# Attention and a state-space convolution in one planned kernel: planner slack, the last chunk in halves, and more filler matmuls

## The chip, the cores and the metric

The kernel runs on one core of a Trainium2 chip. The metric is device time in microseconds. The core has five engines with an instruction queue each: TensorE (PE, with its weight loads shown as PEld), VectorE (DVE), ScalarE (ACT), GpSimd (POOL) and SyncE (SP). They meet through semaphores. Here POOL and SP issue the DMAs.

## The reference

Two results are mixed by a gate for each of 2048 tokens: `g * a + (1 - g) * b`, where `g` is the sigmoid of `x · gate_w`. All inputs are bf16.

```python
# a: attention, 16 heads of 28, one shared key and value head, D = 448
q = (x @ wq).reshape(B, S, H, Dh).transpose(0, 2, 1, 3)
k = x @ wk
v = x @ wv
p = softmax(einsum("bhqd,bkd->bhqk", q, k) * Dh ** -0.5)
a = einsum("bhqk,bkd->bhqd", p, v).transpose(...).reshape(B, S, H * Dh) @ wo
# b: a long convolution of u = x with K, 448 channels, 256 complex states each
P = exp((dt * A)[:, :, None] * arange(L))
K = einsum("dn,dnl,dn->dl", Cc, P, dt * Bc).real
b = causal_convolution(u, K) + u * Dskip
```

Both parts are applied to the same `x`. The reference convolves through FFTs, the kernel multiplies Toeplitz matrices.

## The kernel before

**Attention.** There are 16 steps, called heads here: four blocks of 512 queries by four groups of four heads. A head has 64 score tiles (16 key blocks by 4 heads), each 128x512, so 1024 tiles in all. `qk` (L1110) makes three or two tiles at a time in PSUM, ScalarE takes their exponential into a ring `expT` (L1126), and `pv` (L1135) multiplies four tiles by the values; a column of ones gives the softmax denominators. ScalarE has this stream and little else.

**Normalisation.** When a head is complete, `norm` has VectorE copy the accumulator out of PSUM into `acc` (L1025, two buffers). Then POOL issues four DMAs that gather the denominators into `denT`, VectorE takes the reciprocal (L1030), POOL issues one DMA to a DRAM scratch `R_scratch` and four that broadcast it back into `rdenB`, and VectorE multiplies `acc` by it into `onT` (L1034). The last head goes through matmuls instead (L1042, L1053). `outp` and `tail` project `onT` and `fold` adds into the output `O` (L1016).

**Convolution.** The 448 channels are 14 chunks of 32, in blocks of 2, 4, 4 and 4 chunks. For a block, `masters` makes powers in float32 and stores bf16 copies in `mbf`. For a chunk, `tables` makes powers by doubling on VectorE, in five levels (L885 to L891: two products, a subtraction and an addition each), then a real factor `rho` (L898), their product (L902) and a negation (L907). `kgen` multiplies the tables on TensorE (L924) into 32 rows of K, VectorE adds the skip term and casts to `kstg` (L934, L937), and POOL issues nine DMAs into `KP_scratch`. `tload` then reads, from SP, one Toeplitz tile `T` for each four channels (1072 KB, a ring of five, called groups 0 to 111 in the text). `conv` runs for 16 channels at a time, so twice a chunk, over four groups: 128 matmuls (L970), a product with the gate into `cst` on VectorE (L979), a shift and transpose by matmuls (L990), and an addition into `O` (L998).

**What sets the order.** `Prog.schedule` plans all instructions ahead with its own estimate of each one's length, takes the one that can start soonest, and fixes one order for each engine. Engines then run in that order: an instruction that waits holds everything behind it on its engine. A score matmul has priority: other TensorE work is not planned into the last `MARGIN` ns before ScalarE needs new scores. `SLACK` moves the planned ready time of low priority work that depends on another engine, which changes its place in the order and adds no wait. Afterwards `fill` puts matmuls on zeros into TensorE's planned idle time wherever a moving window's score of planned activity is under `SCORE`.

Of the kernel before, what the change touches and what calls it, by code (L numbers as in the profile page):

```python
# [28 lines left out]
BW = 64 * BC  # L29
MC = 1280 + 5 * 64  # L30
NTR = 5
RING = 15
NON = 5
# [38 lines left out]
class Op:  # L72
    __slots__ = ("i", "eng", "fn", "ns", "lat", "deps", "pr", "lock", "unlock", "slot", "ndma",
                 "count", "vc", "end", "comm", "extra", "mode", "st")


class Prog:
# [5 lines left out]
    MARGIN = 120.0  # L83
# [11 lines left out]
    def op(self, eng, fn, ns, rd=(), wr=(), pr=0, lat=None, lock=None, unlock=None, comm=None, mode="f", st=None):  # L95
# [4 lines left out]
        o.mode = mode  # L100
# [43 lines left out]
    def schedule(self):  # L144
# [20 lines left out]
        while done < n:  # L165
# [68 lines left out]
            for j in succ[i]:  # L234
                need[j] -= 1
                x = ops[j]
                if x.eng == e and o.slot is None and e == "pe":
                    t = free[e]
                elif x.eng == e and o.slot is None:
                    t = free[e] + self.SAME[e]  # L240
                else:
                    t = end + self.SEM_NS
                    if x.pr >= (1.2 if x.eng == "pe" else 2):
                        t += self.SLACK.get(x.eng, 0.0)
# [104 lines left out]
def on(i):  # L349
    return i % NON  # L350


class Kernel:
# [3 lines left out]
    SCORE = 13.8  # L357
# [77 lines left out]
    def consts(self):  # L435
# [6 lines left out]
        dm(V(self.kstg, 0, 256), 0.0, 170, ["kst"])  # L442
# [33 lines left out]
    def loads(self):  # L476
# [41 lines left out]
        for k in range(2, 6):  # L518
# [7 lines left out]
               (448, 128), "pad", rd=["kst"], wr=["pad"], pr=3)  # L526
# [164 lines left out]
    def prep_params(self):  # L691
# [8 lines left out]
        tc = lambda j: spot[j][0].v(0, P, spot[j][1], [[D, 2], [32, NC], [1, 32]])  # L700
# [41 lines left out]
        ap9 = self.seed.v(0, P, 2 * W2, [[32, 2], [64, NC], [1, 32]])  # L742
        pg.op("act", lambda e: e.activation(ap9, tc(0), AF.Exp, scale=-2.0), 950, rd=[K(0)], wr=["sq"], pr=0.5)
        zc = lambda c: self.seed.v(0, P, c * W2, [[32, 2], [64, NC], [1, 32]])
        wc = lambda c: self.seedw.v(0, P, c * W2, [[32, 2], [64, NC], [1, 32]])
# [20 lines left out]
        for s in range(2):  # L766
            o = s * LO + 32 * EW
            for comp, val in ((0, 1.0), (1, 0.0)):
                pg.op("dve", lambda e, o=o, comp=comp, val=val: e.memset(self.tab.v(0, P, o + comp * BLK, [[1, 64]]), val), 70,
                      wr=[("lo", s, 0)] + (xd if s == 0 else ["sz0", "sz1", "sq", "sw0", "sw1"]), pr=3)  # L770
# [39 lines left out]
    def masters(self, b):  # L810
# [22 lines left out]
        for k in range(11):  # L833
# [12 lines left out]
            off = k * 256 if k < 5 else (k - 6) * 256 + 64  # L846
            dv(lambda e, k=k, off=off: e.tensor_copy(mbf.v(0, P, off, [[128, 2], [MC, nb], [1, 64]]), both(k, [[64, nb], [1, 64]])),
               2 * w, keys(k) + tp, [("mb", k)], 1.92)
        qq = self.sz.v(0, P, 2 * BW, [[1, w]])
        qd = self.sz.v(0, P, 2 * BW, [[64, nb], [1, 64]])  # L850
        for lv in range(5):
            if lv:
                dv(lambda e: e.tensor_tensor(qq, qq, qq, ALU.mult), w, ["sqq"], ["sqq"])
            dv(lambda e, lv=lv: e.tensor_copy(mbf.v(0, P, 1280 + 64 * lv, [[MC, nb], [1, 64]]), qd), w, ["sqq"] + tp, [("mq", lv)], 1.92)

    def tables(self, c):
# [4 lines left out]
        mo = ci * MC  # L861
        tab, mbf, tmp, rho = self.tab, self.mbf, self.tmp, self.rho
        pr = 50 + 2 * c

        def vo(fn, n, rd, wr, rate=1.92):
            pg.op("dve", fn, el(n, rate), rd=rd, wr=wr, pr=pr)
        mk = lambda lv: [("mb", lv), ("mb", lv + 6)]
        lk = lambda l: ("lo", s, l)
        vo(lambda e: e.tensor_copy(tab.v(0, P, lo + 31 * EW, [[BLK, 2], [1, 64]]), mbf.v(0, P, mo, [[128, 2], [1, 64]])),
           128, [("mb", 0), lk(0)], [lk(1)])  # L870
        vo(lambda e: e.tensor_copy(tab.v(0, P, lo + 31 * EW + 64, [[BLK, 2], [1, 64]]),
                                   self.sw.v(0, P, ci * 64, [[BW, 2], [1, 64]])),
           128, ["sbw", "sbw2", lk(0)], [lk(2)])
        done = [lk(1), lk(2)]
        for lv in range(5):
            w = 1 << lv
            m = mo + lv * 256
            n = w * EW
            so, do = lo + (32 - w) * EW, lo + (32 - 2 * w) * EW
            src = tab.v(0, P, so, [[BLK, 2], [EW, w], [1, EW]])  # L880
            dst = tab.v(0, P, do, [[BLK, 2], [EW, w], [1, EW]])
            mr = mbf.v(0, P, m, [[0, 2], [0, w], [1, EW]])
            mi = mbf.v(0, P, m + 128, [[0, 2], [0, w], [1, EW]])
            kr, ki = lk(3 + 2 * lv), lk(4 + 2 * lv)
            vo(lambda e, dst=dst, src=src, mr=mr: e.tensor_tensor(dst, src, mr, ALU.mult), 2 * n, done + mk(lv), [kr, ki])  # L885
            tb, to, tk = (tmp, 0, "tmp") if lv < 4 else (tab, FM, "Fm")
            vo(lambda e, src=src, mi=mi, w=w, tb=tb, to=to: e.tensor_tensor(  # L887
                tb.v(0, P, to, [[w * EW, 2], [EW, w], [1, EW]]), src, mi, ALU.mult), 2 * n, done + mk(lv), [tk])
            vo(lambda e, do=do, n=n, tb=tb, to=to: e.tensor_tensor(  # L889
                tab.v(0, P, do, [[1, n]]), tab.v(0, P, do, [[1, n]]), tb.v(0, P, to + n, [[1, n]]), ALU.subtract), n, [tk, kr], [kr])  # L890
            vo(lambda e, do=do, n=n, tb=tb, to=to: e.tensor_tensor(  # L891
                tab.v(0, P, do + BLK, [[1, n]]), tab.v(0, P, do + BLK, [[1, n]]), tb.v(0, P, to, [[1, n]]), ALU.add), n, [tk, ki], [ki])
            done = done + [kr, ki]
        vo(lambda e: e.tensor_copy(rho.v(0, P, 31 * 64, [[1, 64]]), mbf.v(0, P, mo + 1280, [[1, 64]])), 64,
           [("mq", 0)], ["tmp"])
        for lv in range(5):
            w = 1 << lv
            vo(lambda e, w=w, lv=lv: e.tensor_tensor(rho.v(0, P, (32 - 2 * w) * 64, [[64, w], [1, 64]]),  # L898
                                                     rho.v(0, P, (32 - w) * 64, [[64, w], [1, 64]]),
                                                     mbf.v(0, P, mo + 1280 + 64 * lv, [[0, w], [1, 64]]), ALU.mult), w * 64,  # L900
# [319 lines left out]
```

## Time and profile before

| what | us |
|---|---|
| median of 13 runs | 560.27 |
| lowest and highest | 550.6, 566.21 |
| the profiled execution, its own time | 556.17 |
| its span, first to last instruction | 554.4 |
| mean granted TensorE clock in it | 0.892 |

The profile is of one execution. Busy times of an engine are unions of its instructions' times; a group's mean is the length of one instruction; "idle before" is the engine's idle time just before such instructions, with what ended most of it. These groups matter:

```profile
L1126 ACT ACTIVATE expT<-psS 128x1536 bf16<-128x1536 f32 (+1 forms) x410 | 468.9, 1324 | 28.4 <-PE psS L1110 27.0
L1110 PE MATMUL psS<-qT,kT 29*128 29x512 bf16 x1024 | 176.8, 422 | 29.6 <-ACT expT L1126 25.1
L885 DVE TENSOR_TENSOR tab<-tab,mbf 128x256 bf16<-128x256 bf16 (+4 forms) x70 | 68.7, 981 | 1.0
L902 DVE TENSOR_TENSOR tab<-tab,tmp 128x4096 bf16<-128x4096 bf16 x14 | 32.0, 2288 | 0.3
```

Read the first line so: 410 exponentials kept ScalarE busy 468.9 us, the mean one took 1324 ns, and ScalarE was idle 28.4 us before them, 27.0 of that until scores from L1110 were ready. The DMA issues, with the median time from issue to landing:

```profile
T<-KP_scratch SPq DMA_DIRECT2D x112, 1072.0 KB, 9.5
rdenB<-R_scratch POOLq DMA_DIRECT2D x60, 64.0 KB, 5.6
KP_scratch<-kstg POOLq DMA_DIRECT2D x112, 16.0 KB, 3.6
```

### The profile page before, as it was taken

To read this page: it belongs to the slowest core of one execution; us is meant where nothing else is said; L and a number is where in the kernel's file an instruction comes from. 1 tells how busy PE (TensorE), PEld (TensorE's weight loads), DVE (VectorE), ACT (ScalarE), POOL (GpSimd) and SP (SyncE) were. 2 spreads that over 40 slices of the span, in tenths; PEclk is the share of its full clock that TensorE was granted. 3 is DMA by queue.
4 is the path that set the end of the run, shared out by engine and by line. 5 is a ranking of instruction groups with operands and counts; after the bars stand their busy time and mean duration, and the time that the engine had idled before them with its cause. 6 is when DMAs were issued, how large, how long until landed. Compare 5 with 4: busy or idle time off the path is not lost.

```text
span 554.4 us, 19990 instructions
## 1 busy us (share of the span) xinstructions
PE 484.1 (87%) x9080; PEld 259.4 (47%) x9080; DVE 460.9 (83%) x870; ACT 483.4 (87%) x427; POOL 139.9 (25%) x281
## 2 busy tenths in 40 slices
PE   6789979889797989989998989988998989899852
PEld 5545344446354544545354544444454534445541
DVE  7979799998989899999989898998999798911230
ACT  2899899999999989999998989999899989879700
POOL 2000111512214244024213144213313141415000
PEclk9975588799799999999787998899799999869985
DMA  8931100594767778998774878897793979877994
GB/s 237 271 115 48 31 21 4 155 402 146 281 253 270 314 287 290 350 379 312 281 301 138 354 278 316 266 411 310 241 422 80 371 261 352 309 273 246 343 424 160
DMA packets 37628, 142.81 MB, mean 258 GB/s; under 512 B 9888, under 2 KB 20680, under 8 KB 23208
## 3 DMA queue, kind: packets, MB, share of 16 engines
q1 hardware_dynamic: 27656, 135.29, 65.0%
q0 software_dynamic: 8352, 6.09, 4.6%
q8 instruction: 71, 1.16, 0.8%
q10 hardware_dynamic: 1536, 0.17, 0.4%
q14 instruction: 13, 0.11, 0.1%
HBM read 135.38 MB, written 5.74 MB: 255 GB/s over the span
## 4 chain that ended last, share of the span: by engine, by line
DVE 41%; PE 23%; DMA 18%; ACT 12%; POOL 3%; issue 2%; SPq 0%
ACT expT L1126 12%; DMA denT<-acc 11%; PE psS L1110 7%; DVE tab L885 6%; PE psB L1135 4%; DMA T<-KP_scratch 4%; DVE tab L889 4%; DVE tab L887 4%; DVE tab L891 3%; DVE tab L902 3%; POOL denT L134 3%; DVE tmp L887 3%; DVE tmp L898 3%; PE psS L970 2%; DVE cst L979 2%
## 5 line engine op out<-in xcount | busy, mean ns | idle before, releaser
L1126 ACT ACTIVATE expT<-psS 128x1536 bf16<-128x1536 f32 (+1 forms) x410 | 468.9, 1324 | 28.4 <-PE psS L1110 27.0
L1110 PE MATMUL psS<-qT,kT 29*128 29x512 bf16 x1024 | 176.8, 422 | 29.6 <-ACT expT L1126 25.1
L1135 PE MATMUL psB<-expT,vaug 128*32 128x512 bf16 x1024 | 111.7, 427 | 0.3 <-DVE acc L1025 0.3
L1110 PEld LDWEIGHTS psS<-qT,kT 29*128 29x128 bf16 x1024 | 41.3, 93 | 101.5 <-ACT expT L1126 71.8
L134 POOL DMA_DIRECT2D denT<-acc x60 | 29.9, 504 | 207.3 <-DVE acc L1025 115.1
L134 POOL DMA_DIRECT2D KP_scratch<-kstg x126 | 67.5, 544 | 44.0 <-DVE kstg L937 38.3
L885 DVE TENSOR_TENSOR tab<-tab,mbf 128x256 bf16<-128x256 bf16 (+4 forms) x70 | 68.7, 981 | 1.0
L970 PE MATMUL psX<-T,U 128*18 128x128 bf16 (+7 forms) x1920 | 56.2, 247 | 7.1 <-DMA T<-KP_scratch 5.0
L1135 PEld LDWEIGHTS psB<-expT,vaug 128*32 128x32 bf16 x1024 | 26.6, 94 | 70.0 <-issue 67.1
L970 PEld LDWEIGHTS psX<-T,U 128*18 128x18 bf16 (+7 forms) x1920 | 48.5, 161 | 20.8 <-issue 10.6
L970 PE MATMUL psS<-T,U 128*24 128x128 bf16 (+7 forms) x1664 | 47.9, 251 | 4.2 <-issue 1.6
L970 PEld LDWEIGHTS psS<-T,U 128*24 128x24 bf16 (+7 forms) x1664 | 41.3, 161 | 16.5 <-issue 10.9
L924 PE MATMUL psS<-tab 128*32 128x64 bf16 x1152 | 44.2, 288 | 1.0 <-DVE tab L889 1.0
L134 POOL DMA_DIRECT2D rdenB<-R_scratch x60 | 30.4, 513 | 39.3 <-DMA R_scratch<-denT 39.2
L924 PEld LDWEIGHTS psS<-tab 128*32 128x32 bf16 x1152 | 33.0, 136 | 9.6 <-issue 5.9
L887 DVE TENSOR_TENSOR tmp<-tab,mbf 128x256 bf16<-128x256 bf16 (+3 forms) x56 | 36.3, 648 | 0.0
L902 DVE TENSOR_TENSOR tab<-tab,tmp 128x4096 bf16<-128x4096 bf16 x14 | 32.0, 2288 | 0.3
L887 DVE TENSOR_TENSOR tab<-tab,mbf 128x4096 bf16<-128x4096 bf16 x14 | 32.0, 2282 | 0.0
L134 POOL DMA_DIRECT2D R_scratch<-denT x15 | 8.7, 578 | 81.2 <-DVE denT L1030 44.8
L924 PE MATMUL psX<-tab 128*32 128x64 bf16 x640 | 25.6, 289 | 3.7 <-DVE tab L891 2.0
L898 DVE TENSOR_TENSOR tmp<-tmp,mbf 128x64 bf16<-128x64 bf16 (+4 forms) x70 | 25.3, 361 | 0.8
L835 DVE TENSOR_TENSOR msq<-sz 128x512 f32<-128x512 f32 (+1 forms) x40 | 24.6, 614 | 0.0
(147 smaller groups left out, 537.1 us busy)
## 6 DMA issues: line engine op xcount, KB each, us to landing
T<-KP_scratch SPq DMA_DIRECT2D x112, 1072.0 KB, 9.5
rdenB<-R_scratch POOLq DMA_DIRECT2D x60, 64.0 KB, 5.6
U<-in_A_x_dram SPq DMA_DIRECT2D x3, 896.0 KB, 14.8
tab<-in_A_x_dram SPq DMA_DIRECT2D x4, 448.0 KB, 7.1
KP_scratch<-kstg POOLq DMA_DIRECT2D x112, 16.0 KB, 3.6
SZ_scratch<-tab SPq DMA_DIRECT2D x1, 1344.0 KB, 5.2
out_dram<-O SPq DMA_DIRECT2D x3, 448.0 KB, 3.8
sz<-SZ_scratch SPq DMA_DIRECT2D x3, 384.0 KB, 3.6
```

What stands on the lines that cost most here:

```text
L134: return [e.dma_start(o, i, **kw) for o, i in pairs]
L835: dv(lambda e, k=k: e.tensor_tensor(two(msq), both(k - 1), both(k - 1), ALU.mult), 2 * w, keys(k - 1), ["msq"])
L885: vo(lambda e, dst=dst, src=src, mr=mr: e.tensor_tensor(dst, src, mr, ALU.mult), 2 * n, done + mk(lv), [kr, ki])
L887: vo(lambda e, src=src, mi=mi, w=w, tb=tb, to=to: e.tensor_tensor(tb.v(0, P, to, [[w * EW, 2], [EW, w], [1, EW]]), src, mi, ALU.mult), 2 * ...
L889: vo(lambda e, do=do, n=n, tb=tb, to=to: e.tensor_tensor(tab.v(0, P, do, [[1, n]]), tab.v(0, P, do, [[1, n]]), tb.v(0, P, to + n, [[1, n]] ...
L898: vo(lambda e, w=w, lv=lv: e.tensor_tensor(rho.v(0, P, (32 - 2 * w) * 64, [[64, w], [1, 64]]), rho.v(0, P, (32 - w) * 64, [[64, w], [1, 64]]),
L902: vo(lambda e: e.tensor_tensor(tab.v(0, P, FM, [[64, 2], [EW, 32], [1, 64]]), tab.v(0, P, lo + 31 * EW, [[BLK, 2], [-EW, 32], [1, 64]]), r ...
L924: r = e.matmul(G.v(32 * g, 32, 64 * jj, [[1, 64]]), tab.v(0, P, lo + comp * BLK + 64 + o, [[EW, 32]]), tab.v(0, P, fo, [[mo - fo, 2], [EW, ...
L970: r = e.matmul(ps.v(32 * j, 32 - 2 * n, 128 * k, [[1, 128]]), self.U.v(0, P, 2 * n * D + 4 * gi + j, [[D, 32 - 2 * n]]), self.T.v(0, P, s ...
L1110: r = e.matmul(self.psS.v(0, P, 512 * (bo + k), [[1, 512]]), kT.v(32 * h, DH + 1, 128 * kt, [[1, 128]]), qT.v(32 * h, DH + 1, 512 * (i % 2 ...
L1126: pg.op("act", lambda e: e.activation(expT.v(0, P, 512 * es, [[1, n]]), self.psS.v(0, P, 512 * bo, [[1, n]]), AF.Exp, scale=SQ), 50 + n / ...
L1135: r = e.matmul(self.psB.v(32 * h, 32, 0, [[1, 512]]), vaug.v(0, P, 32 * kt, [[1, 32]]), expT.v(0, P, 512 * (t % RING), [[1, 512]]), start= ...
```

## The change

Six things change.

- Operations can name their own planned slack `slk`. The reciprocal gets 4000 ns (it had none), the product into `onT` 4000 (300 before), and the casts to `kstg` and `cst` and the addition into `O` 800 (300 before).
- `MARGIN` goes from 120 to 250 ns.
- `SCORE`, the filler's threshold, goes from 13.8 to 17.
- The tables have another layout. A row of 128 columns held 64 columns of plain powers and 64 that carry the seed `sw` (32 channels by two halves of the states in each); now it holds 32 and 32 for the first 16 channels and the same for the second 16, and the copies in `mbf` and the seeds follow it. The last product of `tables` becomes two of half the length in every chunk.
- Chunk 13, the last, runs `tables` and `kgen` twice, for 16 channels each. Each half has its own PSUM bank, its own two casts, its own five DMAs into `KP_scratch` and its own semaphore.
- A T load depends on the half that wrote its channels.

```diff
+HALVES = (13,)
+SLK = (4000, 4000, 800)
...
-    MARGIN = 120.0
+    MARGIN = 250.0
...
-                    if x.pr >= (1.2 if x.eng == "pe" else 2):
-                        t += self.SLACK.get(x.eng, 0.0)
+                    if x.pr >= (1.2 if x.eng == "pe" else 2) or x.slk:
+                        t += self.SLACK.get(x.eng, 0.0) if x.slk is None else x.slk
...
-    SCORE = 13.8
+    SCORE = 17.0
...
-        vo(lambda e: e.tensor_tensor(tab.v(0, P, FM, [[64, 2], [EW, 32], [1, 64]]),
-                                     tab.v(0, P, lo + 31 * EW, [[BLK, 2], [-EW, 32], [1, 64]]),
-                                     rho.v(0, P, 31 * 64, [[0, 2], [-64, 32], [1, 64]]), ALU.mult), 4096,
-           done + ["tmp"], ["Fm"])
+        for h in range(2) if whole else (sub,):
+            vo(lambda e, h=h: e.tensor_tensor(tab.v(0, P, FM + 32 * h, [[64, 2], [EW, 32], [1, 32]]),
+                                              tab.v(0, P, lo + 31 * EW + 64 * h, [[BLK, 2], [-EW, 32], [1, 32]]),
+                                              rho.v(0, P, 31 * q + (32 * h if whole else 0), [[0, 2], [-q, 32], [1, 32]]), ALU.mult),
+               2048, done + ["tmp"], [("Fm", h)])
...
-              el(504), rd=[X], wr=["kst2"], pr=2, unlock=G)
+              el(504), rd=[X], wr=k2, slk=SLK[2], pr=2, unlock=G)
...
-               (128, 2 * TW), f"T{s}", rd=[("KP", gi // 8), "pad"] + x, wr=[("T", s)], pr=1, extra=2500)
+               (128, 2 * TW), f"T{s}", rd=[("KP", gi // 4), "pad"] + x, wr=[("T", s)], pr=1, extra=2500)
...
-              el(512), rd=[X, "omq"], wr=[ck], pr=2)
+              el(512), rd=[X, "omq"], wr=[ck], pr=2, slk=SLK[2])
...
-            pg.op("dve", lambda e: e.reciprocal(dv, dv), 160, rd=["dn"], wr=["dn"], pr=1)
+            pg.op("dve", lambda e: e.reciprocal(dv, dv), 160, rd=["dn"], wr=["dn"], pr=1, slk=SLK[0])
...
-                  el(512), rd=[ak, "rd", "onw"], wr=[("on", on(i))], pr=2)
+                  el(512), rd=[ak, "rd", "onw"], wr=[("on", on(i))], pr=2, slk=SLK[1])
...
-                self.tables(c)
-                self.kgen(c)
+                for sub in (0, 1) if c in HALVES else (None,):
+                    self.tables(c, sub)
+                    self.kgen(c, sub)
```

Since the planner sees new ready times, the order of all engines changes, not only around these lines.

## The prediction

> **What bounds the kernel now.** First the page's busy times and its sliced clock.
>
> ```profile
> span 554.4 us, 19990 instructions
> PE 484.1 (87%) x9080; PEld 259.4 (47%) x9080; DVE 460.9 (83%) x870; ACT 483.4 (87%) x427; POOL 139.9 (25%) x281
> PEclk9975588799799999999787998899799999869985
> ```
>
> No engine is full over the span, and TensorE's granted clock dips again and again. The chain of waits says which work paced whom.
>
> ```profile
> DVE 41%; PE 23%; DMA 18%; ACT 12%; POOL 3%; issue 2%; SPq 0%
> ```
>
> ScalarE only does exponentials, yet it holds 12% of the chain: VectorE paces the middle. In the chain's next line the largest DMA is "denT<-acc", 11% or 61 us: the chain goes through a normalisation transfer at ten heads. The busy times by stage show where ScalarE is short of work (columns: window, length, then busy time of PE, PEld, DVE, ACT, POOL, then granted clock, DMA share, GB/s).
>
> ```profile
> 35.00:73.00 38.00, 37.74 (x433) 17.98 (x435) 32.09 (x89) 33.64 (x29) 4.21 (x9) 0.51 0.10 31
> 73.00:140.00 67.00, 58.38 (x1148) 30.78 (x1143) 63.37 (x128) 65.74 (x60) 16.92 (x34) 0.92 0.43 150
> 140.00:250.00 110.00, 99.04 (x1967) 52.68 (x1959) 104.88 (x189) 105.34 (x93) 32.40 (x63) 0.95 0.83 307
> 250.00:350.00 100.00, 92.42 (x1780) 47.56 (x1781) 92.35 (x171) 93.98 (x83) 33.61 (x64) 0.89 0.77 281
> 350.00:450.00 100.00, 90.48 (x1881) 48.17 (x1873) 93.13 (x170) 95.62 (x84) 29.07 (x56) 0.95 0.81 304
> 480.00:497.00 17.00, 15.24 (x217) 6.24 (x217) 7.29 (x11) 12.02 (x11) 3.64 (x8) 0.60 0.78 290
> ```
>
> The exponentials run from 26.6 to 523.0 us and keep ScalarE busy 468.9 us, so about 27.5 us are idle. Length minus ACT by stage: 4.4, 1.3, 4.7, 6.0, 4.4 and 5.0; in the stage between the last two rows, 450 to 480, it is 1.7 (28.29 busy). VectorE is 93 to 95% full from 140 to 450. The totals of the waits name what stops it.
>
> ```profile
> ACT expT L1126 <- PE psS L1110: 27.0, 38, 2.0
> DVE denT L1030 <- DMA denT<-acc: 23.4, 11, 6.3
> DVE onT L1034 <- DMA rdenB<-R_scratch: 8.8, 3, 7.3
> ```
>
> VectorE stands still until a transfer lands, with the tables queued behind. The timelines of VectorE, TensorE and ScalarE around 470 us show the sequence.
>
> ```profile
> 470.08 0.25 DVE L1030 RECIPROCAL denT<-denT 128x16 f32<-128x16 f32 x1 [1.94 <-DMA denT<-acc]
> 481.04 0.45 PE L990 MATMUL psX<-ident,cst 128*64 128x64 bf16 x16 [1.01 <-DVE cst L979]
> 483.40 3.78 ACT L1126 ACTIVATE expT<-psS 128x1536 bf16<-128x1536 f32 x3 [1.89 <-PE psS L1110]
> ```
>
> VectorE loses 1.94 us, later TensorE waits for VectorE, the scores come late, ScalarE loses 1.89; then the clock falls to 0.60 and four more gaps of 0.4 to 1.05 us follow by 496. Last, the end of the chain:
>
> ```profile
> 531.17 12.66 DMA T<-KP_scratch
> 543.88 1.13 PE psX L970 x17
> ```
>
> The last T load is issued at 531.2 and lands 12.7 us later; 407 to 433 GB/s flow from 526 to 540, so the end is a queue of T loads.
>
> **Reciprocal and product moved later.** In the order of VectorE's instructions I count the work queued between the copy of the accumulator (L1025) and the reciprocal (L1030), with this trace's start-to-start times by shape: 5.4 to 7.2 us for most heads before, 9.2 to 11.7 after (2.8 for the last). From the end of the copy to the reciprocal it took 7.0 to 8.9 us at the ten stalled heads between. So the queue now covers the transfer (POOL's 1.5 us of issue and 5 to 7 us of flight). The stalls that go: the ten reciprocals from 130.7 to 470.1 us stood 1.69, 1.42, 1.83, 1.09, 1.48, 1.02, 1.11, 2.47, 2.99 and 1.94, sum 17.0; two products stood 0.59 and 0.91; together 18.5 us. The stalls of 6.35 and 7.28 at 502 and 521 us had no table work behind them and count for nothing. What is late next: POOL issues R_scratch and rdenB some 3 us later, and head 5 took 14.3 us between copy and reciprocal, so one or two stalls may stay. Products follow the reciprocal by 18 to 28 us of queued work (13 to 23 before), against about 15.5 us at head 12.
>
> **The longer planned delay for cst, kstg and the O addition** (300 to 800 ns) and the larger margin before scores (120 to 250) move no work, only places: convolutions start 5 to 35 score tiles later in the middle, and the last chunk ends at the same tile, 980. No instruction is added. From both sides: TensorE's waits for cst, 7.6 us in all, bound a gain; the same sum is the loss if the places are worse. I take zero, keeping both ends.
>
> **New layout and halves.** VectorE gets 915 instructions for 870: 13 whole chunks split the last product (+13), chunk 13 runs everything twice (+32). The row at 256 columns has 284 ns, at 512 it has 422; two halves cost 2×284−422=146 ns more by duration, about 70 ns by start-to-start time, since records overlap by 80. So 44×0.07=3.1, and the second kstg cast is not halved, +0.6: 3.7 us, bound above by 44×0.146+0.6=7.0. Cover: the 18.5 us of stalls that go; without it, it is 3.7 us on VectorE. No bf16 operation here has rows of 32; the float products L729 with rows of 32 take 1082 ns, with long rows 1081 to 1092, so zero; the upper bound, were the negation L907 (686 ns for 1984) to run at L891's 1218 for 2048, is 14×0.5=7 us. One more POOL issue is 0.5 us beside idle POOL.
>
> **Net on the exponentials.** VectorE gains 18.5−3.7=14.8 us. Of ScalarE's idle time 21.8 us lie from 140 to 497, downstream of such lateness, so VectorE's gain is the smaller bound; I take 85% of it, because of heads like 5: −12.5 us. Ends: 0 and −21.8.
>
> **Clock, row against rule.** From 35 to 73 us PE is busy 37.74 of 38 us and the clock stays at 0.51; filler there hardly grows (room is gone), so I take nothing. From 450 to 480 the clock was 1.00, and after TensorE's pauses of 1.01 and 0.75 us it was 0.60; I let the clock follow the pauses. The Trainium skill, "TensorE: Matmul & The Clock Gate", section "What's actually happening", lets one busy window of about 3.4 us restore full speed; by it the first stage's 4.4 us could go too, and the sum would be 4.4 lower. Its section "Why this matters for your kernels" lets only gaps over about 3 us throttle; that speaks against this change, since removing 1 us waits would then leave the clock alone, and by it I would take half of the 12.5.
>
> **Filler score 17.** By the order, filler units (one 128x128 matmul or a group of four 32-column ones) go from 375 to 585, 141 of the 210 added after score tile 300. Eight units took 0.85 us at half clock, so 0.106 each, and half of that by the clock ratio at full. They are put where the plan leaves TensorE idle: cost zero while that room exists; without it 141×0.053=7.5 to 210×0.106=22 us.
>
> **The end.** Chunk 13's first half is multiplied at tiles 943 to 950 rather than 965, and written by five issues. Before, its four T loads issued at 517.9 to 520.6, after the write landed; now each waits only for its ring slot, so from the order: 513.4, 517.2, 519.5, 522 on the old clock. The next two are issued about 2 and 3 us earlier, because the convolution of group 103 moves ahead of the first output projections; the last two about 2.5 later, as all projections precede group 105. At 2.6 us a load (538.75 to 541.35 to 543.88) and 5.7 at least for a lone one, the last lands at 539 to 541.5 against 543.8. I take −3; ends −6 (share of 25.9 us for eight loads above 8×2.6=20.8, and one) and +3.
>
> **Sum.** 554.4−12.5−3.0=538.9 of span; 1.8 lie outside it (556.17−554.4): 540.7. The profiled run was 4.1 under the median 560.27: 544.8, so **545 us**. Its own range, 533 to 552, is idle time down to the 5.7 us before 140 and −6 at the end, or half the gain.
>
> **Rivals.** *Filler takes the place* (12%): the added units sit in front of score matmuls when TensorE runs behind its plan. For it: PE is busy 90 to 93% from 250 to 450, and at half clock in the first stage 100%. Against it: ScalarE's gaps there mostly follow waits for VectorE. It decides once over half the units fall on the path with the stalls unhealed: 560.3+7.5 to +22 less 3, 565 to 579, so 570. *The wait moves* (14%): VectorE stays late, now for later products and cst work, and only the end gains: 560.3−3=557. For it: 44.8 us of POOL's waits were already for the reciprocal. Against it: the queue counts above. *Halves do nothing* (inside the forecast): the ring slots, not the write, hold the loads; 548.
>
> The forecast has 74%. A measurement here tells about 1% from no change. The range 532 to 566 leaves out some 6% below and 9% above. Faster by over 1% (under 554.7): 0.74; within 1% (to 565.9): 0.15; slower: 0.11.
>
> **What would show it.** VectorE's wait for denT<-acc under 10 us, nearly all in the end; ScalarE's wait for psS near 14; clock above 0.92; exponentials ending near 510; the last T load landing some 18 us after them (20.9 before). It is wrong if that wait is gone and ScalarE still idles over 20 us, or if filler matmuls stand before the gaps.

## The result and the profile after

| | before | after |
|---|---|---|
| median, us | 558.19 (48 runs) | 575.63 (11 runs) |
| lowest and highest, us | 550.6, 566.21 | 562.31, 586.18 |
| profiled execution, us | 556.17 | 573.01 |
| its span, us | 554.4 | 571.2 |
| its mean granted clock | 0.892 | 0.843 |

The ratio of after to before is 1.0169 (95% interval 1.0133 to 1.0206): slower, where 545 us was forecast. The ratio compares only the runs of each kernel within 1.5% of its own fastest, so where runs spread, as here from 562 to 586 us, it lies nearer to 1 than the medians do; the profiled execution, 573.01 us, is outside that band, so the page below shows a larger loss (16.8 us of span) than the ratio (some 9.5 us). I weigh kernels against each other by their ratios.

The first lines of the changed kernel's page, its busy times, its clock and its chain of waits by engine:

```profile
span 571.2 us, 21007 instructions
PE 517.8 (91%) x9566; PEld 281.7 (49%) x9566; DVE 467.6 (82%) x915; ACT 486.3 (85%) x427; POOL 139.7 (24%) x282
...
PEclk9857655559998996999899995898999999868875
...
PE 44%; ACT 30%; DMA 10%; DVE 10%; POOL 2%; issue 2%; ACTq 0%
```

The chain has turned over. VectorE, 41% of it before, is at 10%, and TensorE has gone from 23% to 44%; its busy time grew by 33.7 us, VectorE's by 6.7. The clock line has a run of fives where before it had two.

The stages that the prediction showed, in the changed kernel (window, length, busy time of PE, PEld, DVE, ACT, POOL, granted clock, DMA share, GB/s):

```profile
35.00:73.00 38.00, 35.36 (x430) 16.82 (x433) 30.43 (x89) 33.26 (x29) 2.14 (x4) 0.63 0.10 29
73.00:140.00 67.00, 66.52 (x980) 32.82 (x968) 56.36 (x111) 58.57 (x51) 13.82 (x27) 0.58 0.40 144
140.00:250.00 110.00, 102.58 (x2122) 55.86 (x2119) 104.04 (x188) 106.02 (x94) 35.29 (x68) 0.94 0.74 264
250.00:350.00 100.00, 90.68 (x1812) 48.07 (x1810) 92.89 (x178) 93.84 (x83) 29.45 (x57) 0.95 0.79 292
350.00:450.00 100.00, 95.29 (x1937) 50.38 (x1935) 93.45 (x179) 95.04 (x84) 29.03 (x56) 0.91 0.77 287
480.00:497.00 17.00, 16.35 (x302) 9.44 (x296) 15.34 (x40) 15.15 (x15) 5.37 (x11) 0.91 0.83 314
```

From 73 to 140 us TensorE is busy for 66.52 of 67 us at a clock of 0.58, and ScalarE does 58.57 us of work where it did 65.74 before: 7.2 us less in a stage that had lost only 1.3. In the three stages from 140 to 450 ScalarE works as long as before, within 0.7 us. Another kernel with the same plan there (u_half below, the change with chunk 13 whole, 562.2 us of span) has the same in this stage: 59.17 us of exponentials at a clock of 0.62.

The totals of the waits in the changed kernel (engine, line, waited for: us, times, longest):

```profile
ACT expT L1141 <- PE psS L1125: 36.7, 54, 1.4
...
DVE acc L1040 <- PE psB L1150: 14.2, 7, 8.6
```

No wait of VectorE for "denT<-acc" is left, after 23.4 us before: the stall that the forecast removes is gone. The work queued between the copy and the reciprocal now takes 9.7 to 11.6 us for all but the last heads, as the prediction counted. ScalarE's wait for scores nevertheless rose from 27.0 to 36.7 us, and VectorE now waits for TensorE.

Parts of the end of the chain (start, length, what):

```profile
487.37 3.40 DMA KP_scratch<-kstg
490.82 1.52 PE psX L938 x21
...
511.26 1.92 PE psS L938 x32
...
552.04 8.54 DMA T<-KP_scratch
560.63 1.14 PE psX L985 x32
```

Both halves of chunk 13 are multiplied on the chain, the second from 511 us on, although its tables are complete at 506.4. The exponentials end at 537.6 us (522.9 before), and 33.5 us follow them (31.5 before). So most of the loss lies inside the exponentials.

### The profile page after: what moved, and what is told of

The parts are those of the page before. It is cut to its first block, busy times and chain, and to the rows that moved or that the text cites. A ratio compares the mean times of both kernels' runs of the same rounds, so it can differ in the third digit from the quotient of the medians.

```text
span 571.2 us, 21007 instructions
## 1 busy us (share of the span) xinstructions
PE 517.8 (91%) x9566; PEld 281.7 (49%) x9566; DVE 467.6 (82%) x915; ACT 486.3 (85%) x427; POOL 139.7 (24%) x282
## 4 chain that ended last, share of the span: by engine, by line
PE 44%; ACT 30%; DMA 10%; DVE 10%; POOL 2%; issue 2%; ACTq 0%
ACT expT L1141 30%; PE psS L1125 13%; PE psB L1150 8%; PE psX L938 4%; DMA T<-KP_scratch 4%; DMA KP_scratch<-kstg 3%; PE psS L938 3%; PE psS L985 3%; PE psX L985 3%; POOL KP_scratch L137 2%; PE psB L633 2%; DMA sz<-SZ_scratch 2%; DMA sz<-in_A_wv_dram 2%; PE psB L626 2%; PE psX L798 1%
## 5 line engine op out<-in xcount | busy, mean ns | idle before, releaser
L1141 ACT ACTIVATE expT<-psS 128x1536 bf16<-128x1536 f32 (+1 forms) x410 | 471.5, 1299 | 40.1 <-PE psS L1125 36.7
L1125 PE MATMUL psS<-qT,kT 29*128 29x512 bf16 x1024 | 185.4, 439 | 21.4 <-ACT expT L1141 15.6
L893 DVE TENSOR_TENSOR tab<-tab,mbf 128x256 bf16<-128x256 bf16 (+5 forms) x75 | 69.4, 927 | 1.1
L985 PE MATMUL psX<-T,U 128*20 128x128 bf16 (+7 forms) x1792 | 55.9, 256 | 6.7 <-DMA T<-KP_scratch 4.6
L985 PEld LDWEIGHTS psX<-T,U 128*24 128x24 bf16 (+7 forms) x1792 | 47.5, 160 | 20.2 <-issue 11.5
L985 PE MATMUL psS<-T,U 128*18 128x128 bf16 (+7 forms) x1792 | 52.1, 246 | 1.3 <-issue 1.2
L985 PEld LDWEIGHTS psS<-T,U 128*18 128x18 bf16 (+7 forms) x1792 | 44.6, 161 | 11.7 <-issue 8.7
L895 DVE TENSOR_TENSOR tmp<-tab,mbf 128x256 bf16<-128x256 bf16 (+4 forms) x62 | 39.4, 635 | 0.0
L633 PE MATMUL psB<-ident,zero 128*32 128x128 bf16 x996 | 34.1, 261 | 1.2 <-issue 1.2
L912 DVE TENSOR_TENSOR tab<-tab,tmp 128x2048 bf16<-128x2048 bf16 x28 | 33.7, 1219 | 0.3
L633 PEld LDWEIGHTS psB<-ident,zero 128*32 128x32 bf16 x996 | 25.4, 116 | 12.6 <-issue 9.4
L907 DVE TENSOR_TENSOR tmp<-tmp,mbf 128x64 bf16<-128x64 bf16 (+5 forms) x75 | 26.0, 347 | 1.0
```

The costliest lines, as they stand in the source:

```text
L633: r = e.matmul(t.v(32 * j, 32, bo, [[1, 128]]), self.zero.v(0, P, 0, [[1, 32]]), self.ident.v(0, P, 0, [[1, P]]), start=not acc, stop=Fals ...
L895: vo(lambda e, src=src, mi=mi, w=w, n=n, tb=tb, to=to: e.tensor_tensor(tb.v(0, P, to, [[n, 2], [cw, w], [1, cw]]), src, mi, ALU.mult), 2 * ...
L912: vo(lambda e, h=h: e.tensor_tensor(tab.v(0, P, FM + 32 * h, [[64, 2], [EW, 32], [1, 32]]), tab.v(0, P, lo + 31 * EW + 64 * h, [[BLK, 2], ...
L985: r = e.matmul(ps.v(32 * j, 32 - 2 * n, 128 * k, [[1, 128]]), self.U.v(0, P, 2 * n * D + 4 * gi + j, [[D, 32 - 2 * n]]), self.T.v(0, P, s ...
L1125: r = e.matmul(self.psS.v(0, P, 512 * (bo + k), [[1, 512]]), kT.v(32 * h, DH + 1, 128 * kt, [[1, 128]]), qT.v(32 * h, DH + 1, 512 * (i % 2 ...
L1141: pg.op("act", lambda e: e.activation(expT.v(0, P, 512 * es, [[1, n]]), self.psS.v(0, P, 512 * bo, [[1, n]]), AF.Exp, scale=SQ), 50 + n / ...
```

## The experiments

All are edits of one of the two kernels. "End" is the time from the last exponential to the end of the span, and "T loads" are those issued after it; both are read from each run's trace, and so is the time at half clock (the granted clock is either 0.5 or 1.0 in these traces, and the fractions in the stages are means). The last three columns are of one profiled execution of each kernel.

| kernel | median, us (runs) | ratio to before | exponentials end, end, T loads | half clock before 140 us, us | mean clock |
|---|---|---|---|---|---|
| before | 558.19 (48) | 1 | 522.9, 31.5, 4 | 48 | 0.892 |
| after | 575.63 (11) | 1.0169 [1.0133, 1.0206] | 537.6, 33.5, 5 | 96 | 0.843 |
| p_score | 559.24 (12) | 0.9964 [0.9930, 0.9998] | 526.8, 30.9, 4 | 58 | 0.884 |
| p_margin | 559.25 (10) | 0.9965 [0.9919, 1.0012] | 521.6, 30.3, 3 | 48 | 0.906 |
| p_slk | 575.16 (12) | 0.9986 [0.9926, 1.0047] | 538.1, 39.1, 7 | 101 | 0.814 |
| p_layout | 575.01 (4) | 1.0267 [1.0215, 1.0318] | 532.5, 38.9, 7 | 44 | 0.846 |
| p_split | 569.09 (4) | 1.0168 [1.0120, 1.0216] | 528.0, 39.1, 7 | 68 | 0.860 |
| p_half | 586.83 (6) | 1.0424 [1.0355, 1.0492] | 550.4, 34.7, 6 | 82 | 0.813 |
| u_half | 565.59 (10) | 1.0152 [1.0068, 1.0236] | 528.8, 33.4, 5 | 99 | 0.859 |
| u_score | 563.58 (12) | none | 530.7, 30.9, 4 | 82 | 0.855 |
| s_only | 562.84 (10) | 1.0026 [0.9985, 1.0067] | 510.0, 50.3, 11 | 58 | 0.887 |
| n_rec | 545.77 (4) | 0.9757 [0.9690, 0.9824] | 510.3, 33.7, 5 | 72 | 0.892 |
| a_rec | 555.65 (4) | 0.9900 [0.9822, 0.9978] | 524.3, 31.7, 6 | 65 | 0.886 |
| full_b | 555.35 (4) | 0.9839 [0.9781, 0.9897] | 515.8, 31.3, 4 | 6 | 0.934 |
| full_a | 552.90 (4) | 0.9803 [0.9736, 0.9871] | 527.0, 33.6, 5 | 49 | 0.898 |
| s_full | 555.47 (10) | 0.9919 [0.9868, 0.9969] | 501.7, 48.7, 11 | 3 | 0.949 |
| c_rec | 538.27 (4) | 0.9624 [0.9558, 0.9689] | 503.9, 33.6, 5 | 24 | 0.938 |
| c_cst | 560.77 (10) | 0.9985 [0.9942, 1.0028] | 516.0, 36.2, 7 | 7 | 0.932 |
| c_early | 545.15 (4) | 0.9751 [0.9690, 0.9812] | 512.2, 32.0, 3 | 24 | 0.929 |
| n_early | 553.86 (4) | 0.9861 [0.9771, 0.9950] | 521.9, 31.9, 3 | 72 | 0.877 |

**The filler score and the margin, each alone on the kernel before.**

```diff
-    SCORE = 13.8
+    SCORE = 17.0
```

> The kernel before with the filler score raised to 17, nothing else. Theory F: 1 to 3% slower than before, longer half-clock stretch before 140 us (48 us of half clock in before's profile, 96 in the change's). Theory O: within 0.5% of before.

```diff
-    MARGIN = 120.0
+    MARGIN = 250.0
```

> The kernel before with the margin at 250, nothing else: another order of the same instructions, with no part of the layout. Theory O (any new order can move the time by some per cent, since the clock reacts to it): off before by more than 1% either way. Theory C or F without O: within 1% of before.

Both give 559.2 us, ratios 0.9964 and 0.9965: theory O of the first text and the "within 1%" of the second. Neither costs anything by itself. Taking the score back in the changed kernel is another matter:

```diff
-    SCORE = 17.0
+    SCORE = 13.8
```

> The change with the filler score put back to 13.8, nothing else: the same order of all other instructions. Theory F (the added filler lowers TensorE's clock and delays the scores): ratio to before 0.97 to 0.99, half-clock time within the exponentials under 100 us (153 in the profile of the change), ScalarE idle near 25 us. Theory O (the new order of the side work is worse, filler is not to blame): ratio within 0.5% of the change's 1.017, half-clock time still above 130 us.

The median falls from 575.6 to 563.6. The runs spread from 551 to 576 us and no ratio came of them, so the 12 us are a difference between two sets of runs that overlap; I take the sign from them, not the size. The trace does not show theory F's mechanism: half clock within the exponentials is 143 us, where under 100 was asked (153 in the change), and ScalarE is idle 34.0 us, not near 25.

**The layout, and what in it costs.** p_layout has the changed `tables` and `kgen` on whole chunks, with the old score, margin and delays (the edit is against the change):

```diff
-HALVES = (13,)
+HALVES = ()
-SLK = (4000, 4000, 800)
+SLK = (0, 300, 300)
-    MARGIN = 250.0
+    MARGIN = 120.0
-    SCORE = 17.0
+    SCORE = 13.8
```

> The new table layout alone, with the last chunk whole and the old slack, margin and score. If the halves are what cost the two-halves kernel 27 us: within 1% of before. If the layout (its matmuls or the order that the planner makes of it) costs it: 3 to 5% slower than before.

Its ratio is 1.0267, some 15 us of 560. p_split keeps the old layout and only makes the last product in two pieces of 2048, which gives the same order of operations as p_layout on every engine:

```diff
...
-        vo(lambda e: e.tensor_tensor(tab.v(0, P, FM, [[64, 2], [EW, 32], [1, 64]]),
-                                     tab.v(0, P, lo + 31 * EW, [[BLK, 2], [-EW, 32], [1, 64]]),
-                                     rho.v(0, P, 31 * 64, [[0, 2], [-64, 32], [1, 64]]), ALU.mult), 4096,
-           done + ["tmp"], ["Fm"])
+        for h in range(2):
+            vo(lambda e, h=h: e.tensor_tensor(tab.v(0, P, FM + 32 * h, [[64, 2], [EW, 32], [1, 32]]),
+                                              tab.v(0, P, lo + 31 * EW + 32 * h, [[BLK, 2], [-EW, 32], [1, 32]]),
+                                              rho.v(0, P, 31 * 64 + 32 * h, [[0, 2], [-64, 32], [1, 32]]), ALU.mult), 2048,
+               done + ["tmp"], [("Fm", h)])
...
```

> The kernel before, in its old table layout, with the last product of the tables in two pieces as in the new one. The planner gives it the very order that the layout-alone kernel has, on every engine. Theory O (the layout cost its 2.7% through the order that the planner made of two pieces): within 1% of the layout-alone kernel, 570 to 580 us. Theory L (the table matmuls read the new layout more slowly, 27 ns apart for 23.5, and thin out TensorE's work): within 1% of before, with the old spacing.

Ratio 1.0168, so about 9 of the 15 us are the order alone: 14 more instructions on VectorE, and a plan that leaves seven T loads after the exponentials instead of four (an end of 39.1 us instead of 31.5). The other 6 us come with the new layout, in the same order. The lines of the table matmuls, first in p_split (uses of two PSUM tiles; busy us, mean ns):

```profile
L925 PE MATMUL psS<-tab 128*32 128x64 bf16 x1152 | 44.3, 289 | 3.7 <-DVE O L999 3.5 <-issue 0.2
...
L925 PE MATMUL psX<-tab 128*32 128x64 bf16 x640 | 24.9, 289 | 0.5 <-issue 0.5
```

and in p_layout:

```profile
L938 PE MATMUL psS<-tab 128*32 128x64 bf16 x1152 | 46.4, 296 | 2.4 <-DVE O L1013 1.7 <-DVE tab L917 0.5
...
L938 PE MATMUL psX<-tab 128*32 128x64 bf16 x640 | 25.6, 294 | 0.0
```

The same 1792 matmuls keep TensorE busy 72.0 us instead of 69.2, the mean one lasting 5 to 7 ns longer; by start times at full clock they follow each other after 26.5 ns on average instead of 24.9. That is 2.8 us directly. Where the rest of the 6 lies is not shown: the two traces also differ in half clock from 140 us to the last exponential, 106 us in p_layout and 65 in p_split, and no run tells whether the layout brings that.

**The halves.** With old delays, margin and score (against p_layout), and in the changed kernel:

```diff
-HALVES = ()
+HALVES = (13,)
```

> The last chunk in two halves and the new layout, with the old slack, margin and score. Both theories: 0 to 1% faster than before, 3 us by the prediction; if the halves or the layout cost VectorE more than 4 us it is slower by that.

```diff
-HALVES = (13,)
+HALVES = ()
```

> The change with the last chunk whole again. If the halves gain 3 us at the end as forecast: 1 to 5 us slower than the change (575 us). If they cost as in the kernel that has them with the old slack (12 us more than the layout alone): 560 to 568.

In the first setting the halves cost 1.0424 against 1.0267, some 9 us, instead of the 3 us of gain. The end is 4.2 us shorter there (34.7 after 38.9), as forecast, but the exponentials end 17.9 us later. VectorE has the same order in both until chunk 13, and p_half is 4.2 us behind by then, so a part of the 17.9 is not the halves; how the rest comes about is not shown. In the second the ratios (1.0169 with, 1.0152 without) do not tell them apart, while the medians differ by 10 us. The end is the same in both (33.5 and 33.4). So they bring nothing in the total, and cost between nothing and 10 us.

**The delays together.** p_slk puts all the delays on p_layout:

```diff
-SLK = (0, 300, 300)
+SLK = (4000, 4000, 800)
```

> The new planned slack and the new table layout, with the last chunk whole, the margin at 120 and the score at 13.8. Theory F: 1 to 3% faster than before, since VectorE no longer stands at the reciprocal. Theory O: 1 to 2% slower than before, since the slack is what moved the order.

Inconclusive: the runs go from 558 to 589 us, the ratio of 0.9986 rests on few of them, and the median is that of p_layout. The same delays on the kernel before, without the layout, tell more (each changed `op` call gets its `slk`, as in the change's diff):

```diff
+SLK = (4000, 4000, 800)
```

> The kernel before with the new planned slack alone: old layout, whole chunk, margin 120, score 13.8. The forecast of the study: 2 to 3% faster, no stall at the reciprocal. Theory C: the stalls go as forecast, but the time follows the clock: under 0.87 mean clock it is slower than before, over 0.90 faster.

The exponentials end at 510.0 us, the reciprocal never stalls, ScalarE's idle time falls from 27.4 to 16.2 us, about as forecast, and the ratio is 1.0026. The gain is spent at the end. The end of the chain in s_only:

```profile
504.54 9.26 DMA T<-KP_scratch
517.01 2.42 PE psS L1076 x6
519.43 1.71 PE psS L1054 x8
521.14 1.12 PE psS L1076 x3
525.99 1.44 PE psS L971 x60
527.43 8.12 DMA T<-KP_scratch
535.60 1.15 PE psX L971 x23
536.76 13.01 DMA T<-KP_scratch
549.81 1.14 PE psS L971 x23
```

Three loads of T are on the chain one behind the other, with output projections (L1076) between the first and the second; the last is issued 26.8 us after the last exponential. In the order of TensorE's instructions, groups 92 to 95 are convolved at score tiles 1000 to 1020 (945 to 983 before), and a T load needs the ring slot of an earlier convolution. Eleven loads come after the exponentials, not four.

**Which delay, and the forecast's first step alone.** In n_rec and c_rec only the reciprocal and the product are delayed, in c_cst only kstg, cst and O. c_rec and c_cst have filler of 128 rows (below), and s_full both delays with it.

```diff
-            pg.op("dve", lambda e: e.reciprocal(dv, dv), 160, rd=["dn"], wr=["dn"], pr=1)
+            pg.op("dve", lambda e: e.reciprocal(dv, dv), 160, rd=["dn"], wr=["dn"], pr=1, slk=SLK[0] if i < 16 else None)
...
-                  el(512), rd=[ak, "rd", "onw"], wr=[("on", on(i))], pr=2)
+                  el(512), rd=[ak, "rd", "onw"], wr=[("on", on(i))], pr=2, slk=SLK[1] if i < 16 else None)
```

Here `i` is the head, 0 to 15, so all heads have the delay.

> Kernel before, with only the 4000 ns delay for the reciprocal and the product; filler matmuls of 32 rows as before. This is the first step of the forecast alone. If the delay and the filler's rows gain separately (538.3 with both, 555.4 with the rows alone, 559.4 with neither): exponentials end near 510, 33 us after them, 541 to 548. If the delay gains only at the better clock: 550 to 558, exponentials end at 515 to 522 with over 60 us of half clock in the first 140 us.

545.77 us, ratio 0.9757: the forecast's number from its first step alone. In n_rec the wait of ScalarE for scores, and the chain by engine:

```profile
ACT expT L1127 <- PE psS L1111: 15.6, 25, 1.2
```

```profile
ACT 55%; PE 26%; DVE 14%; DMA 2%; issue 1%; ACTq 0%; SPq 0%
```

and the end of its chain:

```profile
463.18 46.65 ACT expT L1127 x41
...
519.46 2.02 PE psX L971 x84
521.52 11.94 DMA T<-KP_scratch
533.50 1.14 PE psS L971 x17
```

ScalarE paces the kernel: 46.65 us of exponentials stand on the chain in one piece. One T load is on the chain at the end, where s_only had three. s_only differs from n_rec by the 800 ns delay alone; its exponentials end at the same time, and its end is 16.6 us longer. Six more T loads at the prediction's 2.6 us are 15.6.

In the changed kernel, a_rec takes out only that delay, in three places like this one:

```diff
-              el(512), rd=[X, "omq"], wr=[ck], pr=2, slk=SLK[2])
+              el(512), rd=[X, "omq"], wr=[ck], pr=2)
```

> The changed kernel without the 800 ns delay for kstg, cst and O; all else as changed. If that delay is what costs, as the pair of runs on the kernel before showed at the end (33.6 us after 48.7): 555 to 563. If layout, halves and filler cost the 17 us whatever the delay: 571 to 578, since the end of the changed kernel is 33.5 us already.

The ratio falls from 1.0169 to 0.9900, by some 15 us (the medians differ by 20, the lowest runs by 10): without this delay the change is 1% faster than the kernel before. Here the place is another: the end hardly moves (31.7 after 33.5), and the last convolutions stand at the same score tiles in both (965, 990 and 1015); the exponentials end 13.3 us sooner. The first stages in a_rec:

```profile
35.00:73.00 38.00, 35.07 (x476) 16.82 (x476) 34.22 (x90) 35.04 (x31) 2.63 (x5) 0.66 0.10 30
73.00:140.00 67.00, 64.43 (x1099) 33.12 (x1099) 59.21 (x126) 61.73 (x54) 16.30 (x33) 0.73 0.42 150
```

Up to score tile 260 ScalarE is idle 8.6 us, against 14.9 in the changed kernel, 15.7 in u_half and 6.9 before. It is tempting to say that the delay pushes convolutions out of this stage, since from 73 to 140 us a_rec starts 220 convolution matmuls and 323 filler matmuls, the changed kernel 128 and 378. But a window in time counts fewer of them in a kernel that is late: in the order of TensorE the second 128 convolution matmuls stand at score tile 220 in a_rec and before, at 215 in the changed kernel, and up to tile 180 both have the same 677 filler matmuls (601 before). What the traces do show is more half clock before 140 us, 96 us against 65. The five traces with the 800 ns delay on the new layout (after, u_half, u_score, p_slk, full_a) have 14 to 19 us of idle ScalarE up to tile 260, the three without it (p_layout, p_half, a_rec) 6 to 11, and s_only, with it on the old layout, 6. Which displaced instruction does this stays open.

The delays one by one with the filler held at 128 rows: c_rec has n_rec's two lines, c_cst three like this one.

```diff
-              el(512), rd=[X, "omq"], wr=[ck], pr=2)
+              el(512), rd=[X, "omq"], wr=[ck], pr=2, slk=SLK[2])
```

> Kernel before, with the 4000 ns delay for the reciprocal and the product in all heads (the 800 ns delay for kstg, cst and O left out) and filler matmuls of 128 rows. Compared with both delays and the same filler (555.5, end after the exponentials 48.7 us) and with no delay and the same filler (555.4, 31.3 us). Theory A, the delay of normalisation itself pushes the last convolutions back: end after the exponentials above 42 us, exponentials end near 503, 550 to 556. Theory B, the 800 ns delay does it: end near 32 us, exponentials end near 503, 536 to 545. The plan lies between the two (convolution groups 92 to 95 at score tiles 975 to 985, after 945 to 983 without and 1000 to 1020 with both), so an end of 35 to 42 us would be a share of each.

> Kernel before, with only the 800 ns delay for kstg, cst and the O addition, and filler matmuls of 128 rows. Theory A, this delay costs nothing at the end: 31 us after the exponentials, 553 to 557 as with the filler alone. Theory B, it pushes the last convolutions back and gains nothing before: end 38 to 46 us, the exponentials end near 516 with reciprocal stalls of 17 us as before, 558 to 565.

c_rec has ratio 0.9624, c_cst 0.9985, full_b (neither delay) 0.9839, s_full (both) 0.9919. The 800 ns delay costs 0.0146 on full_b and 0.0295 on c_rec, 8 and 16.5 us: with either filler it takes away what the other delay brings, and more when the exponentials end sooner. Theory B holds; the end of c_cst, 36.2 us, was less long than it asked.

**The rows of the filler.** The filler multiplies zeros, in groups of four matmuls of 128 rows by 32 columns (192 matmuls from 35 to 73 us in the kernel before) and in single ones of 32 rows by 128 columns (73 there). This edit gives the single ones all 128 rows, at the same places in the order (full_b on the kernel before, full_a on the changed one, s_full on s_only):

```diff
-                        r = e.matmul(t.v(0, P, bo, [[1, 128]]), self.zero.v(0, 32, 0, [[1, P]]), self.ident.v(0, 32, 0, [[1, P]]),
+                        r = e.matmul(t.v(0, P, bo, [[1, 128]]), self.zero.v(0, P, 0, [[1, P]]), self.ident.v(0, P, 0, [[1, P]]),
```

> The kernel before with the same edit to its 32-row filler. Theory C: half clock in the first 140 us falls from 48 to under 30 us, 0.5 to 1.5% faster than before. Theory F: 0 to 1% slower.

> The change, with the 32-row filler matmuls between scores made 128 rows tall: as many filler matmuls in the same places, four times the array cells each. Theory C (the clock follows the array cells in use, and the half-speed stretches, of random length, are what the change lost by): half clock in the first 140 us falls from 96 to under 30 us, mean clock above 0.90, time 545 to 558. Theory F (filler occupies TensorE and delays scores): no better than the change, 570 to 580.

> The new slack alone with 128-row filler. Theory C: clock above 0.92 and the recovered VectorE time is kept: 535 to 548 us, faster than the kernel before with 128-row filler (555 us). Theory F or O: no better than 555.

The kernel before gains 1.6% by it, the changed one falls from 1.0169 to 0.9803, some 20 us, and s_full gains 1.1% on s_only; its exponentials end at 501.7 us, but the end of 48.7 us stays, so its 555.5 us miss theory C's 535 to 548 while its clock of 0.949 is theory C's. The first stages of full_b:

```profile
35.00:73.00 38.00, 32.02 (x525) 15.52 (x524) 36.89 (x97) 38.00 (x35) 4.70 (x9) 1.00 0.12 37
73.00:140.00 67.00, 59.12 (x1142) 29.94 (x1131) 63.96 (x125) 65.12 (x58) 18.68 (x36) 0.95 0.47 164
```

The row from 35 to 73 us had a clock of 0.51, TensorE busy 37.74 us and 33.64 us of exponentials before; now the clock is 1.00 with TensorE busy for less, and ScalarE is never idle. In all five pairs with the same order and the two kinds of filler, half clock before 140 us falls: 48 to 6 us (before, full_b), 96 to 49 (after, full_a), 58 to 3 (s_only, s_full), 72 to 24 (n_rec, c_rec) and 72 to 24 (n_early, c_early).

full_a keeps 49 us of it, where theory C asked for under 30; its traced execution, 562.47 us, was the slowest of its four. Its trace shows that ScalarE's idle time goes with the half clock. Score tiles 60 to 180, first in the changed kernel, then in full_a, which has the same order:

```profile
60.00:125.00 65.00, 64.66 (x827) 30.24 (x823) 56.20 (x108) 56.73 (x49) 14.01 (x27) 0.50 0.23 78
62.00:117.00 55.00, 48.05 (x856) 23.47 (x852) 52.44 (x96) 55.00 (x50) 14.02 (x27) 1.00 0.26 85
```

At half clock ScalarE is idle 8.3 us here, at full clock not at all. In full_a the half clock comes back at tiles 180 to 220, 20 us of it with 6.4 us of idle ScalarE, so up to tile 260 it loses 14.5 us, as much as the changed kernel; in this trace its gain lies behind that tile.

**Keeping the end as it was.** c_early delays reciprocal and product for heads 0 to 11 only, with MARGIN 250 and the filler of 128 rows; n_early is the same with 32 rows.

```diff
-            pg.op("dve", lambda e: e.reciprocal(dv, dv), 160, rd=["dn"], wr=["dn"], pr=1)
+            pg.op("dve", lambda e: e.reciprocal(dv, dv), 160, rd=["dn"], wr=["dn"], pr=1, slk=SLK[0] if i < 12 else None)
```

> Kernel before, with the 4000 ns delay for the reciprocal and the product of heads 0 to 11 only, no 800 ns delay, MARGIN 250, filler matmuls of 128 rows. The plan puts the last convolutions where the kernel before has them (groups 92 to 99 at score tiles 945 to 995). If the gain of the delay was lost at the end only: exponentials end at 501 to 506, 30 to 34 us after them, 535 to 545. If the gain is lost wherever it arises (another wait takes it): exponentials end near 515, 552 to 557.

> The same with the 32-row filler of the kernel before. If array cells in the filler set the clock and the delay is a separate gain: 8 to 15 us slower than with 128 rows, 545 to 556, with 40 us or more of half clock in the first 140 us. If the clock of the early stage does not matter once the delay is right: within 3 us of it.

The totals came in as expected, 545.2 and 553.9, but the exponentials of c_early end at 512.2, not 501 to 506: with heads 12 to 14 left as they were, 7.5 us of reciprocal stalls return and 9.5 of the 19.2 us of ScalarE's idle time fall after score tile 900 (0.1 of 11.7 in c_rec). The end was a little better (32.0 us after 33.6), the last stretch of the exponentials worse. c_rec, with every head delayed, stays the best kernel of the study. The first lines of its page:

```profile
span 537.5 us, 20109 instructions
...
PE 471.3 (88%) x9133; PEld 257.2 (48%) x9148; DVE 461.8 (86%) x870; ACT 480.2 (89%) x427; POOL 140.4 (26%) x281
...
PEclk9955999999998699997999999999999999999985
```

## Why the prediction was wrong

**Its own sign of being wrong came:** the wait for denT<-acc is gone, and ScalarE still idles 39.0 us, not under 20.

**Reciprocal and product moved later: right.** n_rec is this step alone. The stalls of 18.5 us went, the exponentials end at 510.3 (forecast near 510), ScalarE's wait is 15.6 us (near 14), and the kernel takes 545.77 us. That this equals the forecast's 545 is luck: the forecast also holds 3.7 us of cost for layout and halves and a gain of 3 us at the end, which n_rec does not have, and its end is 2.2 us longer. (One reading was off: VectorE is 92 to 95% full from 140 to 450, not 93 to 95; nothing hangs on it.)

**The longer planned delay for cst, kstg and O: the step that failed.** The prediction said that it and the margin "move no work, only places", and "I take zero", with 7.6 us to either side. The runs show some 15 us: 1.0026 against 0.9757 on the kernel before, 1.0169 against 0.9900 in the changed one, and 16.5 with more filler rows. The bound was taken from the wrong row. TensorE's waits for cst price a convolution that is late by a little. On the kernel before, what moved was where the last convolutions stand among the score tiles (groups 92 to 95 at 975 in n_rec, at 1000 in s_only), and with them the T loads, at 2.6 us each. The step saw that the last chunk's tables end at the same tile and stopped there; the convolutions of the chunks before it were to be looked up too. In the changed kernel the same delay costs its 15 us within the exponentials, with 31 us more half clock before 140 us, and by which instruction stays open. The margin alone is indeed worth nothing that can be told.

**New layout and halves: sized on one engine.** VectorE's busy time grew by 6.7 us, near the upper bound of 7.0 rather than the 3.7 taken, and none of its rows got slower. But the split product alone costs 1.7% through the plan, and the table matmuls read the new layout more slowly, which no sentence of the prediction asked. The halves were given a gain of 3 us at **the end**; in the changed kernel they change the end by 0.1 us, and with the old delays they shorten it by 4.2 us and still cost 9 in all.

These parts do not add: layout and halves cost 24 us with the old delays (1.0424), while a_rec, which has them with the filler score and the margin, stands only 8 us above n_rec (0.9900 to 0.9757). Taken in one order, each ratio against the one before it, the steps are n_rec −13.6, then layout, halves, score and margin +8.0, then the 800 ns delay +15.1. They add up to the measured +9.5 (0.0169 of 560) by construction; in another order the shares would differ.

**Filler score: zero only on the kernel before.** There it is confirmed. In the changed kernel the medians say 12 us, inside the 7.5 to 22 of the case without room, but no ratio bears that size out. The rival *filler takes the place* asked for unhealed stalls, and they were healed; its 565 to 579 holds the measured time without its mechanism as put.

**Clock.** I took nothing for the early stage, and "filler there hardly grows". Up to score tile 180 it grew from 601 to 677 matmuls, and half clock before 140 us went from 48 to 96 us. The filler is not the whole of it, since p_score has 665 there and a_rec 677, with 58 and 65 us of half clock. The rule taken for the later stages, "I let the clock follow the pauses", agrees with the runs: TensorE's longest pause from 140 us to the last exponential is 2.05 us before and 0.96 in n_rec, and half clock in that stretch falls from 55 to 27 us; with filler of 128 rows, full_b to c_rec, from 48 to 24. The mean clock of n_rec is 0.892 all the same, not the 0.92 expected, because before 140 us it has 72 us of half clock instead of 48. The Trainium skill's rule, "TensorE: Matmul & The Clock Gate", section "Why this matters for your kernels", by which the prediction would have halved the 12.5, names gaps over about 3 us. Here the clock was halved for 55 us of that stretch before, with no pause over 2.05 us, and with the pauses shortened the exponentials end 12.6 us sooner.

## What to carry to other kernels

A planned delay that "adds no wait" is still a change of order: before pricing it, follow every instruction that it displaces to the last stage, and count the transfers that are left when the pacing engine is done. When two kernels are compared stage by stage, count by the place in the order and not by the clock on the wall, or a kernel that is late seems to have less work. Price a step on each engine that it touches and test it alone, because here a gain of 14 us and losses of 8 and 15 stood in one diff, and the gain needed only the two delays of 4000 ns. Where an engine that paces nothing is kept busy for its clock's sake, look at the clock beside the busy time, and not at the busy time alone.

## What the runs showed of the hardware

Keeping TensorE busy did not keep its clock up. From 35 to 73 us the kernel before has it busy for 37.74 of 38 us at a clock of 0.51; with the same order of instructions and 128 rows instead of 32 in the single filler matmuls it is busy for 32.02 us at 1.00. Half clock before 140 us fell from 48 to 6 us, and in the four other pairs by 47 to 55. The Trainium skill, "TensorE: Matmul & The Clock Gate", section "What's actually happening", has the clock follow how busy the engine was and lets one busy window of about 3.4 us restore it. Here some ten such windows in a row did not, and the measurement decides: the rows in use matter, not busy time alone. How the hardware counts them was not measured.

Half clock followed pauses of 1 to 2 us. In the kernel before, TensorE pauses for 1.19 us from 176.3, 2.05 from 330.1 (its longest from 140 us to the last exponential) and 1.35 from 386.8 us, and half clock begins at 178.4, 332.0 and 390.1 us. It did not follow each of them: after 1.10 us from 197.8 and 1.15 from 443.7 the clock stayed full.

Matmuls of 64 columns on the same data in another layout follow each other after 26.5 instead of 24.9 ns on average at full clock, with 32 of the 128 columns of the array each.

The 11 runs of the changed kernel spread by 24 us, and their times follow the mean clock: 562.31 us at 0.878, 586.18 at 0.808.
